# Attention, gated layers and an expert layer on one core: other PSUM banks for the weight fold, two engines to empty the products with v, longer runs in the first loads, and a new plan

## The chip, the cores and the metric

The kernel runs on one core of a Trainium2 chip. The metric is the device time of one execution in microseconds (us). The kernel before was timed three times, and one more execution was profiled.

## What is computed

The reference has three parts, one behind the other.

```python
# attention, batch 4, 12 heads, 448 rows, 64 columns
scores = cap * tanh(scale * q @ k.T / cap)
x = softmax(scores) @ v                 # 1792 x 768 after the heads are put together
# dense part
h = (x @ w1) * (x @ w2) @ w3            # 768 -> 1024 -> 1024
x = h @ w_out                           # 1024 -> 768
# experts: one of 8 for each row, chosen by x @ w_gate + bias[modality]
out = gate * (max(x @ w1[e], 0) @ w2[e])
```

The weights of the dense part come in 64-bit floats and are narrowed on the chip by four integer steps on VectorE.

## The kernel before, in words

There are two stages.

**The planned stage** holds attention and the preparation of the dense weights. Attention works on 24 pairs of heads. For a pair, `load_k`, `load_q` and `load_v` (lines 432 to 447) fetch the rows; k and q go through SyncE's queue (the first q through ScalarE's), v through GpSimd's. In `load_k` and `load_q` the innermost run is one row of 64 floats, 256 bytes. `tr_k` and `tr_q` transpose on TensorE into a PSUM bank of the tag `tr`, which has two banks; `k_out` and `q_out` copy from there. `score` (line 481) writes two banks of the tag `sc`, which has two buffers of two banks; ScalarE applies tanh out of PSUM and then exp. `pv` (line 500) accumulates products with v in the one buffer `pv` of two banks: its two banks hold two halves of the keys, and their sum is the result. `pv_copy` (line 545) copies the first bank to SBUF on ScalarE, and behind it `pv_out` (line 549) adds the second bank on VectorE; `pair_store` writes it to DRAM. `psum` (line 520) adds the exponentials on VectorE and `sum_mm` adds over partitions on TensorE into an `sc` buffer, which `sum_out` copies.

The dense weights: w_out arrives in 8 pieces, is narrowed (`abs1`, `narrow1`), split in a high and a low part (`cast1`, and `sub1` on GpSimd, line 329), and each piece is transposed (`tr_wo`, copied by `wo_copy`) for a product with w_gate (`wo_gate`, read by `wo_split`, line 594), all through `tr` banks. w3 arrives in 16 pieces, is narrowed (`abs_w3`, `conv_w3`) and transposed (`tr_w3`). `fold` (line 635) multiplies w3 with w_out so that the dense part's last two products become one: 16 pieces of two halves, 12 matmuls each. Both halves of a piece share one `sc` buffer, and `fold_out` (line 652) takes each from there to SBUF on VectorE. Some pieces of w1 and w2 are narrowed and stored in this stage too. 30 transposes of the identity (lines 748 to 751) fill TensorE's first microseconds; they hold one `tr` bank until the last of them.

The order of the instructions on each engine is made when the program is built, by the class `Schedule` (line 20), a list scheduler. Each task has an engine or a choice of engines, a cost in ns, a key (its due time, in quarters of a pair), tasks it depends on, and buffers it takes and gives back in rotation; a load has a time on the DMA queue (`dma`). Of the ready tasks the one that can start first is taken, and among equals the one with the smaller key. A TensorE task of the same kind as the one before (64x64 tiles, or full array) has its key lowered by 2.5 (line 85). These costs and keys only make the order; on the chip each engine follows its own order and waits for its true inputs and buffers. GpSimd's order holds the subtractions of line 329 and the issues of `load_v`.

**The second stage** (from line 964 on) is written out by hand: `phase_x12` multiplies x with w1 and w2, both parts of x (high, index 0, and low, index 1) with the high and low parts of the weights, for six slices of the contraction in turn: high by high, low by high, high by low (lines 1000 to 1002). `phase_x2` and the experts (`stage1`, `stage2`) follow. The split of the first x into high and low parts (lines 933 and 935) lies at the end of the planned stage.

Of the kernel before, what the change touches and what calls it, by code (L numbers as in the profile page):

```python
# [8 lines left out]
F32 = mybir.dt.float32  # L9
# [10 lines left out]
class Schedule:  # L20
# [34 lines left out]
    def run(self):  # L55
# [8 lines left out]
        while ready:  # L64
            best = None
            for i in ready:
# [54 lines left out]
def attention_moe_moe_kernel(  # L121
# [292 lines left out]

    raw_qkv = {}

# [15 lines left out]
    def load_k(p):  # L432
        k2 = at2.tile([P, NC, 2, D], F32, name="k2", tag="k2")
        q2 = at2.tile([CP, NC, 2, D], F32, name="q2", tag="q2")
        raw_qkv[p] = (k2, q2)
        for g in range(2):
            nc.sync.dma_start(k2[rows_of(g), 0:NC - g], keys(heads(k, p), g).rearrange("h p c d -> p c h d"))

    def load_q(p):
        eng = nc.sync if p else nc.scalar  # L440
        eng.dma_start(raw_qkv[p][1], heads(q, p).rearrange("h (p c) d -> p c h d", c=NC))

# [102 lines left out]
    def pv_copy(p):  # L545
        pvs[p] = at1.tile([P, S], F32, name="pvs", tag="pvs", bufs=2)
        nc.scalar.copy(pvs[p], pvb[p][:, 0, :S])

    def pv_out(p):
        nc.vector.tensor_tensor(out=pvs[p], in0=pvb[p][:, 1, :S], in1=pvs[p], op=ALU.add)  # L550

    def pair_store(p):
        b, hp = divmod(p, H // 2)
        nc.sync.dma_start(xb[b][P * hp:P * hp + P, :], pvs[p])

# [224 lines left out]
    for c in range(NW):  # L780
        u = c // 2
        key = (4.0 * c + 3) if c < 8 else (10 + 10.0 * c)
        raw, y, un = ("wraw", c), ("y", c), ("unit", u)
# [8 lines left out]
        if c < 8:  # L792
# [3 lines left out]
            for j in range(2):  # L796
                x = add("PE", 320, kg, do(tr_wo, c, j), [cn3[-1], *gate[-1:], *cps[-1:]], take=[tt[j], *([] if j else [("th", "o", c)])], use=[tt[j], y, ("th", "o", c)])
                cps.append(add({'ACT': (500, -300), 'DVE': (560, 0)}, 0, kg, lambda eng, c=c, j=j: wo_copy(c, j, eng), [x], use=[tt[j], ("th", "o", c)]))
            gate.append(add("PE", 1500, kg, do(wo_gate, c), [*cps, wg_in], take=[tp], use=[tp, ("th", "o", c)]))
# [21 lines left out]
    for p in range(NP + 1):  # L821
# [17 lines left out]
        if p:  # L839

            for c in range(3):
                vl[p - 1, c] = add("PE", 770, 4 * p + c + 2.4, do(pv, p - 1, c), [ex[c], joint, vl.get((p - 1, c - 1))],
                                   use=[pk, ("th", p - 1, c), ("v", p - 1)], mode="tiles")
# [51 lines left out]
    for n, (f, g) in enumerate(SWEEP):  # L895
        key = 5.4 * (n + 2) + 3
        raw, r_, h_, w_ = ("w3raw", n), ("w3r", n), ("tr", "w", n), ("w3t", n)
        t = add("SP", 630, key - 3, do(load_w3, n), take=[raw], use=[raw], dma=1456)
        t = add({'ACT': (660, -300), 'DVE': (610, 0)}, 0, key, lambda eng, n=n: abs_w3(n, eng), [t], take=[r_], use=[raw, r_])
# [3 lines left out]
        t = add("PE", 440, key, do(tr_w3, n), [t], take=[h_], use=[r_, h_])  # L903
        t = add({'DVE': (598, 0), 'ACT': (480, 600)}, 0, key - 4, lambda eng, n=n: w3_h(n, eng), [t], take=[w_], use=[h_, w_])
        wl_[n] = t = add("DVE", 600, key - 4, do(w3_l, n), [t], use=[h_, w_])
        lp = add("SP", 630 if g else 0, key - 3, do(part, n), [fs[n - KF]] if g else [], take=[("wst", n)], use=[("wst", n)],
                 lag=0, dma=1092 if g else None)
        for half in range(2):
            fo = ("sc", "f", n)
            late = vl[NP - 2, 2] if n == FN - 1 else None  # L910
            prev = add("PE", 2130, FK(n, half), do(fold, n, half), [t, units[2 * g], units[2 * g + 1], *augs[4 * g:4 * g + 4], prev, late],
                       take=[] if half else [fo], use=[fo, w_, ("unit", 2 * g), ("unit", 2 * g + 1)])
            fe[n, half] = add("DVE", 560, 0, do(fold_out, n, half), [prev, lp], use=[fo, ("wst", n)])
# [74 lines left out]
    def phase_x12(half, bs, hooks):  # L988
        gt = gp.tile([P, 2, KF, HALF], F32R, name="gT", tag="gT")
        units = {}  # L990
        for i, (u, j) in enumerate(ORDER[half]):
# [357 lines left out]
```

## Time and profile before

| quantity | us |
|---|---|
| three timed runs | 958.78, 961.33, 965.59 |
| median | 961.33 |
| the profiled execution | 963.59 |
| its span in the profile | 961.7 |

The profiled execution's own time is 963.59 us. The span runs from its first to its last instruction; 1.9 us lie around it. The profile names engines PE (TensorE's matmuls), PEld (its weight loads), DVE (VectorE), ACT (ScalarE), POOL (GpSimd) and SP (SyncE). Matmuls are pipelined: a row's duration is the way of one matmul through the array, and the next one starts before it ends, so that PE looks busy where matmuls start at half the possible rate. What the engine really does is read from the distance of starts.

### The profile page before, as it was taken

How to read it: one execution, taken by the hardware profiler on the slowest of the kernel's cores; microseconds unless marked ns; L12 is line 12 of the kernel's file. 1: busy time of each engine (PE TensorE's matmuls, PEld its weight loads, DVE VectorE, ACT ScalarE, POOL GpSimd, SP SyncE). 2: the span in 40 equal slices, each digit the busy share in tenths (PEclk: the TensorE clock that was granted, in tenths of full speed). 3: DMA queues.
4: the chain of work that ended last, by engine and by line, in shares of the span. 5: the costliest groups of instructions: out<-in, count | busy, mean ns of one | idle time of the engine just before them, and what ended most of it. 6: DMA issues, size and time to landing. Idle time of an engine off the chain costs nothing. (4 is left out here: it accounts for less than half of the span.)

```text
span 961.7 us, 13900 instructions
## 1 busy us (share of the span) xinstructions
PE 924.1 (96%) x5618; PEld 763.5 (79%) x5618; DVE 469.1 (49%) x671; ACT 374.9 (39%) x447; POOL 241.0 (25%) x211
## 2 busy tenths in 40 slices
PE   8999989999999999999999999999999999999994
PEld 5456555655655799999999999999899899889894
DVE  4999986786675478721006422100653523423410
ACT  4897766776775333231222211211422312322400
POOL 3434211151110112123542441200604212302011
PEclk9899999999999999999999999999999999999998
DMA  9767785477544565626622341310671591782401
GB/s 225 206 167 219 203 243 141 129 217 179 156 140 121 146 193 164 186 79 215 171 93 96 78 120 34 115 50 33 166 178 43 184 172 33 199 148 52 160 20 44
DMA packets 126088, 132.73 MB, mean 138 GB/s; under 512 B 60926, under 2 KB 107416, under 8 KB 126021
## 3 DMA queue, kind: packets, MB, share of 16 engines
q1 hardware_dynamic: 112644, 114.35, 42.3%
q0 software_dynamic: 12464, 17.22, 7.9%
q8 instruction: 46, 0.75, 0.3%
q10 hardware_dynamic: 912, 0.23, 0.1%
q14 instruction: 22, 0.17, 0.1%
HBM read 102.13 MB, written 30.19 MB: 138 GB/s over the span
## 5 line engine op out<-in xcount | busy, mean ns | idle before, releaser
L1001 PE MATMUL acc<-xT,wh 128*128 128x448 f32 x384 | 141.4, 368 | 0.7 <-DVE xT L935 0.7
L1000 PE MATMUL acc<-xT,wh 128*128 128x448 f32 x384 | 140.4, 366 | 1.5 <-ACT xT L933 1.5
L1002 PE MATMUL acc<-xT,wl 128*128 128x448 f32 x384 | 140.4, 366 | 0.0
L329 DVE TENSOR_TENSOR wl<-raw,wh 128x1536 fp32r<-128x1536 f32 (+1 forms) x42 | 73.6, 1759 | 116.8 <-ACT wh L252 116.8
L252 ACT CAST wh<-raw 128x1536 fp32r<-128x1536 f32 (+1 forms) x48 | 70.3, 1479 | 105.4 <-DMA raw<-in_moe_w_dram 78.5
L487 PE MATMUL sc<-QT,KT 64*64 64x448 f32 x672 | 92.9, 561 | 7.9 <-ACT smt L252 4.2
L507 PE MATMUL pv<-th,vt 64*64 64x448 f32 x672 | 89.2, 551 | 0.0
L498 ACT ACTIVATE th<-th,capb 128x448 f32<-128x448 f32 (+1 forms) x96 | 89.0, 956 | 0.6
L1214 PE MATMUL acc<-wh,hT 128*124 128x384 f32 x256 | 87.8, 343 | 1.1 <-DVE y L1222 0.7
L447 POOL DMA_DIRECT2D vt<-in_v_dram x96 | 50.9, 545 | 146.3 <-PE pv L507 144.9
L1216 PE MATMUL acc<-wh,hT 128*124 128x384 f32 x256 | 86.5, 338 | 0.7 <-DVE hT L1185 0.7
L1215 PE MATMUL acc<-wl,hT 128*124 128x384 f32 x256 | 86.3, 337 | 0.5 <-DVE wl L329 0.5
L1010 POOL TENSOR_TENSOR gT<-a,gT 128x896 fp32r<-128x896 f32 x16 | 43.8, 2740 | 144.2 <-DVE gT L1009 138.7
L1000 PEld LDWEIGHTS acc<-xT,wh 128*128 128x128 f32 x384 | 72.5, 189 | 8.2 <-ACT xT L933 2.3
L1001 PEld LDWEIGHTS acc<-xT,wh 128*128 128x128 f32 x384 | 72.6, 189 | 7.0 <-DVE xT L935 1.2
L492 ACT ACTIVATE th<-sc,icap 128x896 f32<-128x896 f32 x72 | 71.2, 1010 | 16.2 <-PE sc L487 15.6
L1002 PEld LDWEIGHTS acc<-xT,wl 128*128 128x128 f32 x384 | 72.6, 189 | 5.3
L1032 PE MATMUL acc<-wh,gT 128*128 128x388 f32 x224 | 76.4, 341 | 0.0
L1033 PE MATMUL acc<-wl,gT 128*128 128x388 f32 x224 | 76.0, 339 | 0.0
L1034 PE MATMUL acc<-wh,gT 128*128 128x388 f32 x224 | 75.9, 339 | 0.0
L1180 PE MATMUL acc<-xsT,wh 128*128 128x496 f32 x192 | 74.9, 390 | 0.0
L1182 PE MATMUL acc<-xsT,wl 128*128 128x496 f32 x192 | 74.5, 388 | 0.0
(163 smaller groups left out, 1630.1 us busy)
## 6 DMA issues: line engine op xcount, KB each, us to landing
raw<-in_moe_w_dram SPq DMA_DIRECT2D x48, 768.0 KB
w3raw<-in_moe_w_dram SPq DMA_DIRECT2D x16, 512.0 KB
raw<-w_scr SPq DMA_DIRECT2D x8, 776.0 KB
raw<-in_moe_w_out_dram SPq DMA_DIRECT2D x8, 768.0 KB
w_scr<-y SPq DMA_DIRECT2D x16, 384.0 KB
raw<-w_scr SPq DMA_DIRECT2D x8, 768.0 KB
x_scr<-pvs SPq DMA_DIRECT2D x24, 224.0 KB
xraw<-x_scr SPq DMA_DIRECT2D x4, 1344.0 KB
```

The source lines that it names most:

```text
L487: mm(sc[rows_of(side(p, j, g)), g, :S], lhsT=KT[p][rows_of(j), o:o + D], rhs=QT[p][rows_of(j), :], start=True, stop=True)
L498: nc.scalar.activation(tht[p, c], tht[p, c], ACTF.Exp, scale=capb)
L507: mm(pvb[p][rows_of(j), r, :S], lhsT=vt[p][rows_of(r), NC * g + c, :], rhs=tht[p, c][rows_of(r), g, :] if c < NB else tht[p, c][rows_of(r) ...
L1000: mm(acc[:, ft, :S], lhsT=wh[:, o:o + P], rhs=x[:, 0, d, :], start=(d == 0), stop=False)
L1001: mm(acc[:, ft, :S], lhsT=wh[:, o:o + P], rhs=x[:, 1, d, :], start=False, stop=False)
L1002: mm(acc[:, ft, :S], lhsT=wl[:, o:o + P], rhs=x[:, 0, d, :], start=False, stop=(d == KD - 1))
L1032: mm(acc[:, hf, :HA], lhsT=gt[:, 0, f, ts], rhs=wh[:, o:o + HA], start=(f == 0), stop=False)
L1033: mm(acc[:, hf, :HA], lhsT=gt[:, 0, f, ts], rhs=wl[:, o:o + HA], start=False, stop=False)
L1034: mm(acc[:, hf, :HA], lhsT=gt[:, 1, f, ts], rhs=wh[:, o:o + HA], start=False, stop=(f == KF - 1))
L1214: mm(acc[:TP, hf, :HT], lhsT=ht[:, 0, f, cs], rhs=wh[:, o:o + HT], start=(f == 0), stop=False)
L1215: mm(acc[:TP, hf, :HT], lhsT=ht[:, 0, f, cs], rhs=wl[:, o:o + HT], start=False, stop=False)
L1216: mm(acc[:TP, hf, :HT], lhsT=ht[:, 1, f, cs], rhs=wh[:, o:o + HT], start=False, stop=(f == KF - 1))
```

## The change

The fold takes one `tr` bank for each half in place of an `sc` buffer for both. `pvs` has two halves: ScalarE copies one bank of `pv`, the new `pv_copy1` copies the other on VectorE, and `pv_out` adds the two in SBUF on GpSimd. For the first two pairs k and q are loaded head by head with four rows in a run (1024 bytes; 768 for the shorter part of k) into tiles of the tag `th`, and `order_k` (two copies on VectorE) and `order_q` (one on ScalarE) bring them into the old order. In `phase_x12` the products with the low part of x come after the others of a slice of columns. Keys, costs and dependences of the plan change.

```diff
                 if pick[2] == "PE" and self.tasks[i][9] == mode:
-                    key -= 2.5
+                    key -= 1.7
...
+        if p < NF:
+            runs[p] = [at1.tile([P, 2, NC, D], F32, name="run", tag="th", bufs=7) for _ in range(2)]
         for g in range(2):
-            nc.sync.dma_start(k2[rows_of(g), 0:NC - g], keys(heads(k, p), g).rearrange("h p c d -> p c h d"))
+            n, src = NC - g, keys(heads(k, p), g)
+            if p < NF:
+                nc.sync.dma_start(runs[p][0][rows_of(g), :, 0:n], src.rearrange("h p c d -> p h c d"))
+            else:
+                nc.sync.dma_start(k2[rows_of(g), 0:n], src.rearrange("h p c d -> p c h d"))
...
+    def order_k(p):
+        for g in range(2):
+            n = NC - g
+            nc.vector.tensor_copy(raw_qkv[p][0][rows_of(g), 0:n], runs[p][0][rows_of(g), :, 0:n].rearrange("p h c d -> p c h d"))
+
+    def order_q(p):
+        nc.scalar.copy(raw_qkv[p][1], runs[p][1][0:CP].rearrange("p h c d -> p c h d"))
...
     def pv_copy(p):
-        pvs[p] = at1.tile([P, S], F32, name="pvs", tag="pvs", bufs=2)
-        nc.scalar.copy(pvs[p], pvb[p][:, 0, :S])
+        pvs[p] = at1.tile([P, 2, S], F32, name="pvs", tag="pvs", bufs=2)
+        nc.scalar.copy(pvs[p][:, 0, :], pvb[p][:, 0, :S])
+
+    def pv_copy1(p):
+        nc.vector.tensor_copy(pvs[p][:, 1, :], pvb[p][:, 1, :S])
 
     def pv_out(p):
-        nc.vector.tensor_tensor(out=pvs[p], in0=pvb[p][:, 1, :S], in1=pvs[p], op=ALU.add)
+        nc.gpsimd.tensor_tensor(out=pvs[p][:, 0, :], in0=pvs[p][:, 0, :], in1=pvs[p][:, 1, :], op=ALU.add)
...
-        if half == 0:
-            both = psa.tile([P, 2, 512], F32, name="sc", tag="sc", bufs=2)
-            fos[n, 0], fos[n, 1] = both[:, 0, :], both[:, 1, :]
-        fo = fos[n, half]
+        fo = fos[n, half] = bank("tr", 2)
...
-        key = (4.0 * c + 3) if c < 8 else (10 + 10.0 * c)
+        key = (6.0 * c + 3) if c < 8 else (10 + 10.0 * c)
...
-                cps.append(add({'ACT': (500, -300), 'DVE': (560, 0)}, ... do wo_copy
+                cps.append(add({'ACT': (500, 600), 'DVE': (560, 0)}, ... do wo_copy
...
-            lk = add("SP", 1260, k0, do(load_k, p), take=[raw], use=[raw], dma=640)
-            lq = add("SP" if p else "ACT", 630, k0 + 0.1, do(load_q, p), [(lk, 0)] if p else [], use=[raw], dma=640)
-            lv = add("POOL", 2800, k0 + 4.0, do(load_v, p), [(lk, 0)], take=[vk], use=[vk], dma=640)
-            t = add("PE", 380, 4 * p - 5.2, do(tr_k, p), [lk], take=[hk], use=[hk, raw])
+            lk = add("SP", 1260, k0, do(load_k, p), ..., dma=700 if first else 2300)
+            lq = add("SP" if p else "ACT", 630, k0 + 0.1, do(load_q, p), ..., dma=700 if first else 2300)
+            if first:
+                lk = add("DVE", 1050, kk, do(order_k, p), [lk], use=[raw, rk])
+                lq = add("ACT", 620, kk, do(order_q, p), [lq], use=[raw, rq])
+            t = add("PE", 380, 4 * p - 4.2, do(tr_k, p), [lk], take=[hk], use=[hk, raw])
...
+            lv = add("POOL", 2500, k0 + 4.0, do(load_v, p), [lk], take=[vk], use=[vk], dma=900)
...
-                vl[p - 1, c] = add("PE", 770, 4 * p + c + 2.4, do(pv, p - 1, c), ...
+                vl[p - 1, c] = add("PE", 770, 4 * p + c + 0.8, do(pv, p - 1, c), ...
...
-            po[p - 1] = add("DVE", 620, 4 * p - 2, do(pv_out, p - 1), [t], use=[pk, ("pvs", p - 1)])
+            t1 = add("DVE", 620, 4 * p - 2, do(pv_copy1, p - 1), [(t, -500)], use=[pk, ("pvs", p - 1)])
+            po[p - 1] = add("POOL", 1200, 4 * p - 2, do(pv_out, p - 1), [t, t1], use=[("pvs", p - 1)])
...
-        key = 5.4 * (n + 2) + 3
+        key = 4.6 * (n + 2) + 3
...
-        t = add({'ACT': (660, -300), 'DVE': (610, 0)}, 0, key, ... abs_w3
+        t = add({'ACT': (660, 0), 'DVE': (610, 0)}, 0, key, ... abs_w3
...
-            fo = ("sc", "f", n)
+            fo = ("tr", "f", n, half)
...
-                    for d in range(KD):
-                        o = d * 256 + ft * P
-                        mm(acc[:, ft, :S], lhsT=wh[:, o:o + P], rhs=x[:, 0, d, :], start=(d == 0), stop=False)
-                        mm(acc[:, ft, :S], lhsT=wh[:, o:o + P], rhs=x[:, 1, d, :], start=False, stop=False)
-                        mm(acc[:, ft, :S], lhsT=wl[:, o:o + P], rhs=x[:, 0, d, :], start=False, stop=(d == KD - 1))
+                    for part in range(2):
+                        for d in range(KD):
+                            o = d * 256 + ft * P
+                            mm(acc[:, ft, :S], lhsT=wh[:, o:o + P], rhs=x[:, part, d, :], start=(d == part == 0), stop=(part == 1 and d == KD - 1))
+                            if part == 0:
+                                mm(acc[:, ft, :S], lhsT=wl[:, o:o + P], rhs=x[:, 0, d, :], start=False, stop=False)
```

## Rows read from the trace of the kernel before

**Rows 1.** Busy time of each engine in stretches, with instruction counts, granted clock, DMA.

```profile
core 0: us, PE busy (x) PEld busy (x) DVE busy (x) ACT busy (x) POOL busy (x), PEclk, DMA share, GB/s
...
20.00:40.00 20.00, 18.77 (x158) 8.72 (x155) 18.64 (x27) 18.25 (x26) 7.70 (x10) 0.91 0.78 216
40.00:60.00 20.00, 19.30 (x165) 9.74 (x169) 19.73 (x30) 18.55 (x27) 7.21 (x7) 0.91 0.67 180
60.00:140.00 80.00, 76.13 (x610) 48.98 (x606) 72.24 (x116) 57.87 (x80) 24.70 (x30) 1.00 0.78 211
140.00:160.00 20.00, 16.86 (x137) 9.96 (x130) 15.13 (x24) 13.71 (x19) 2.80 (x6) 0.91 0.47 147
160.00:300.00 140.00, 134.45 (x1110) 80.61 (x1110) 97.06 (x150) 101.57 (x130) 31.33 (x58) 1.00 0.61 170
...
315.20:320.00 4.80, 4.13 (x11) 3.46 (x12) 3.08 (x3) 1.63 (x2) 0.00 (x0) 0.64 0.83 260
320.00:949.50 629.50, 626.20 (x3258) 584.90 (x3257) 228.62 (x299) 148.04 (x149) 158.93 (x83) 1.00 0.43 118
```

**Rows 2.** Timeline of PE, 238.5 to 255: start, us, form, count.

```profile
238.91 0.98 PE L487 MATMUL sc<-QT,KT 64*64 64x448 f32 x8 [0.53 <-DVE wst L655]
...
245.09 0.60 PE L474 MATMUL tr<-ident,q 112*128 112x112 f32 x4
245.46 0.42 PE L648 MATMUL sc<-wh,w3h 128*128 128x388 f32 x1
...
249.87 0.98 PE L534 MATMUL sc<-sums,sel 64*64 64x448 f32 x8
```

**Rows 3.** Waits of PE, 14 to 317: who, for whom, us in total, times, longest.

```profile
PE sc L487 <- ACT smt L252: 4.2, 3, 3.1
PE tr L619 <- DVE wl L598: 1.9, 2, 1.3
PE acc L1000 <- ACT xT L933: 1.5, 1, 1.5
PE sc L487 <- ACT th L495: 1.4, 2, 0.7
PE sc L648 <- DVE wst L657: 1.4, 2, 1.0
PE sc L487 <- DVE wst L655: 1.3, 3, 0.6
...
PE acc L1001 <- DVE xT L935: 0.7, 1, 0.7
```

**Rows 4.** Timeline of ACT and of PE, 140.5 to 145.

```profile
141.93 0.89 ACT L224 ACTIVATE y<-raw 128x768 f32<-128x768 f32 x1 [3.61 <-DMA raw<-in_moe_w_dram]
...
144.59 0.59 PE L487 MATMUL sc<-QT,KT 64*64 64x448 f32 x2 [3.15 <-ACT smt L252]
```

**Rows 5.** Timeline of PE, 7 to 14.

```profile
7.24 1.17 PE L460 MATMUL tr<-ident,k 128*128 128x128 f32 x4 [2.46 <-DMA k<-in_k_dram]
8.34 3.67 PE L750 MATMUL tr<-ident 128*128 128x128 f32 x16
11.81 0.95 PE L474 MATMUL tr<-ident,q 112*128 112x112 f32 x4
```

**Rows 6.** Groups of VectorE's instructions in the planned stage, by shape.

```profile
L550 DVE TENSOR_TENSOR pvs<-pv,pvs 128x448 f32<-128x448 f32 x24 | 14.8, 615 | 5.5 <-ACT pvs L547 4.3 <-DMA w3raw<-in_moe_w_dram 1.0
...
L254 DVE COPY KT<-tr 128x448 f32<-128x448 f32 x16 | 9.9, 618 | 2.8 <-PE tr L460 1.8 <-PE sc L487 0.9
```

**Rows 7.** Timeline of GpSimd and of VectorE, 33.3 to 37.

```profile
33.95 1.97 POOL L329 TENSOR_TENSOR wl<-y,wh 128x768 fp32r<-128x768 f32 x1 [6.20 <-ACT wh L252]
...
34.16 2.24 DVE L527 TENSOR_TENSOR sums<-sums,th 128x448 f32<-128x448 f32 x1
```

**Rows 8.** Durations of single lines, ns min/median/max, first and last start in us.

```profile
L527 DVE TENSOR_TENSOR sums<-sums,th x24: 608/617/2242, 24.4 to 310.5; 128x448 f32<-128x448 f32 x24
...
L329 POOL TENSOR_TENSOR wl<-y,wh x14: 1811/1920/2656, 23.7 to 212.1; 128x768 fp32r<-128x768 f32 x14
```

More of the change, by code (lines that the diff above doesn't have):

```diff
@@ L413, in attention_moe_moe_kernel @@
     nc.gpsimd.memset(sel, 1.0)
-    raw_qkv = {}
+    raw_qkv, runs = {}, {}
+    NF = 2
     def rows_of(r):
@@ L435, in load_k @@
         raw_qkv[p] = (k2, q2)
+        if p < NF:
+            runs[p] = [at1.tile([P, 2, NC, D], F32, name="run", tag="th", bufs=7) for _ in range(2)]
         for g in range(2):
-            nc.sync.dma_start(k2[rows_of(g), 0:NC - g], keys(heads(k, p), g).rearrange("h p c d -> p c h d"))
-    def load_q(p):
-        eng = nc.sync if p else nc.scalar
-        eng.dma_start(raw_qkv[p][1], heads(q, p).rearrange("h (p c) d -> p c h d", c=NC))
+            n, src = NC - g, keys(heads(k, p), g)
[3 more added lines that the diff above has]
+                nc.sync.dma_start(k2[rows_of(g), 0:n], src.rearrange("h p c d -> p c h d"))
+    def load_q(p):
+        src = heads(q, p)
+        if p < NF:
+            eng = nc.sync if p else nc.scalar
+            eng.dma_start(runs[p][1][0:CP], src.rearrange("h (p c) d -> p h c d", c=NC))
+        else:
+            nc.sync.dma_start(raw_qkv[p][1], src.rearrange("h (p c) d -> p c h d", c=NC))
+    def order_k(p):
[4 more added lines that the diff above has]
+        nc.scalar.copy(raw_qkv[p][1], runs[p][1][0:CP].rearrange("p h c d -> p c h d"))
     def load_v(p):
@@ L797, in attention_moe_moe_kernel @@
                 x = add("PE", 320, kg, do(tr_wo, c, j), [cn3[-1], *gate[-1:], *cps[-1:]], take=[tt[j], *([] if j else [("th", "o", c)])], use=[tt[j], y, ("th", "o", c)])
-                cps.append(add({'ACT': (500, -300), 'DVE': (560, 0)}, 0, kg, lambda eng, c=c, j=j: wo_copy(c, j, eng), [x], use=[tt[j], ("th", "o", c)]))
+                cps.append(add({'ACT': (500, 600), 'DVE': (560, 0)}, 0, kg, lambda eng, c=c, j=j: wo_copy(c, j, eng), [x], use=[tt[j], ("th", "o", c)]))
             gate.append(add("PE", 1500, kg, do(wo_gate, c), [*cps, wg_in], take=[tp], use=[tp, ("th", "o", c)]))
@@ L828, in attention_moe_moe_kernel @@
             k0, kk = 4 * p - 7, 4 * p - 4.0
-            lk = add("SP", 1260, k0, do(load_k, p), take=[raw], use=[raw], dma=640)
-            lq = add("SP" if p else "ACT", 630, k0 + 0.1, do(load_q, p), [(lk, 0)] if p else [], use=[raw], dma=640)
-            lv = add("POOL", 2800, k0 + 4.0, do(load_v, p), [(lk, 0)], take=[vk], use=[vk], dma=640)
-            t = add("PE", 380, 4 * p - 5.2, do(tr_k, p), [lk], take=[hk], use=[hk, raw])
+            first = p < NF
+            rk, rq = [("th", "run", p, i) for i in range(2)] if first else [None] * 2
+            lk = add("SP", 1260, k0, do(load_k, p), take=[raw, rk, rq] if first else [raw], use=[raw, rk] if first else [raw], dma=700 if first else 2300)
+            lq = add("SP" if p else "ACT", 630, k0 + 0.1, do(load_q, p), [(lk, 0)] if p else [], use=[raw, rq] if first else [raw], dma=700 if first else 2300)
+            if first:
+                lk = add("DVE", 1050, kk, do(order_k, p), [lk], use=[raw, rk])
+                lq = add("ACT", 620, kk, do(order_q, p), [lq], use=[raw, rq])
+            t = add("PE", 380, 4 * p - 4.2, do(tr_k, p), [lk], take=[hk], use=[hk, raw])
             kl = add({'DVE': (620, 0), 'ACT': (530, 300)}, 0, kk, lambda eng, p=p: k_out(p, eng), [t], take=[kt], use=[hk, kt])
             t = add("PE", 380, 4 * p - 5.2, do(tr_q, p), [lq], take=[hq], use=[hq, raw])
+            lv = add("POOL", 2500, k0 + 4.0, do(load_v, p), [lk], take=[vk], use=[vk], dma=900)
             last_at2.append(t)
@@ L841, in attention_moe_moe_kernel @@
             for c in range(3):
-                vl[p - 1, c] = add("PE", 770, 4 * p + c + 2.4, do(pv, p - 1, c), [ex[c], joint, vl.get((p - 1, c - 1))],
+                vl[p - 1, c] = add("PE", 770, 4 * p + c + 0.8, do(pv, p - 1, c), [ex[c], joint, vl.get((p - 1, c - 1))],
                                    use=[pk, ("th", p - 1, c), ("v", p - 1)], mode="tiles")
@@ L895, in attention_moe_moe_kernel @@
     for n, (f, g) in enumerate(SWEEP):
-        key = 5.4 * (n + 2) + 3
+        key = 4.6 * (n + 2) + 3
         raw, r_, h_, w_ = ("w3raw", n), ("w3r", n), ("tr", "w", n), ("w3t", n)
         t = add("SP", 630, key - 3, do(load_w3, n), take=[raw], use=[raw], dma=1456)
-        t = add({'ACT': (660, -300), 'DVE': (610, 0)}, 0, key, lambda eng, n=n: abs_w3(n, eng), [t], take=[r_], use=[raw, r_])
+        t = add({'ACT': (660, 0), 'DVE': (610, 0)}, 0, key, lambda eng, n=n: abs_w3(n, eng), [t], take=[r_], use=[raw, r_])
         t = add({'DVE': (500, 0)}, 0, key, lambda eng, n=n: conv_w3(n, 0, eng), [t], use=[raw, r_])
@@ L902, in attention_moe_moe_kernel @@
             t = add("DVE", (0, 425, 690, 910)[i], key, do(conv_w3, n, i), [t], use=[raw, r_])
-        t = add("PE", 440, key, do(tr_w3, n), [t], take=[h_], use=[r_, h_])
-        t = add({'DVE': (598, 0), 'ACT': (480, 600)}, 0, key - 4, lambda eng, n=n: w3_h(n, eng), [t], take=[w_], use=[h_, w_])
+        t = add("PE", 440, key, do(tr_w3, n), [t], take=[h_, w_], use=[r_, h_, w_])
+        t = add({'DVE': (598, 0), 'ACT': (480, 600)}, 0, key - 4, lambda eng, n=n: w3_h(n, eng), [t], use=[h_, w_])
         wl_[n] = t = add("DVE", 600, key - 4, do(w3_l, n), [t], use=[h_, w_])
@@ L908, in attention_moe_moe_kernel @@
         for half in range(2):
-            fo = ("sc", "f", n)
+            fo = ("tr", "f", n, half)
             late = vl[NP - 2, 2] if n == FN - 1 else None
             prev = add("PE", 2130, FK(n, half), do(fold, n, half), [t, units[2 * g], units[2 * g + 1], *augs[4 * g:4 * g + 4], prev, late],
-                       take=[] if half else [fo], use=[fo, w_, ("unit", 2 * g), ("unit", 2 * g + 1)])
+                       take=[fo], use=[fo, w_, ("unit", 2 * g), ("unit", 2 * g + 1)])
             fe[n, half] = add("DVE", 560, 0, do(fold_out, n, half), [prev, lp], use=[fo, ("wst", n)])
```

2 lines of the change are left out of this document (1 added, 1 removed).

## The prediction

> **What bounds the kernel now.** The first view to read is the busy time in stretches. In the second stage TensorE has work in 626.2 of 629.5 us at a granted clock of 1.00 [rows 1]: nothing that the change touches there takes a matmul away, so the second stage stays as long as it is. The planned stage ends at 315.2 us, and all that can be won lies in it. There the busy column deceives. The timeline shows it: from 238.91 to 245.09 TensorE starts 64 tile matmuls, and from 245.46 to 249.87 the 24 matmuls of a fold piece [rows 2], though single rows there show 0.3 to 1 us. So a dense tile matmul costs 6.18 / 64 = 0.097 us and a fold matmul 4.41 / 24 = 0.184 us. The stage has 1536 tile matmuls (24 pairs by 28 + 28 + 8), 384 of the fold (16 by 24) and 400 small ones (transposes and products with w_gate). By the dense rate that is 1536 x 0.0966 = 148.3, 384 x 0.184 = 70.6, and for the small ones 400 x 0.12 = 48, an estimate, since four transposes of q take 0.37 [rows 2] and those of k reach further. Together 267 us. The first transposes of q start at 11.81 [rows 5]; from there to 315.2 are 303 us. About 36 us of the stage are therefore lost on TensorE, and this is the pot.
>
> Two views say where they go. First the clock: in 20:40, 40:60 and 140:160 it was granted at 0.91 [rows 1], each time a part of the stretch at the lower of the two levels, 1.2 GHz; that is (1 - 0.91) x 20 = 1.8 us of work each, 5.4 together. Before the one at 140:160 TensorE had stood for 3.15 us [rows 4]. Second the list of waits: scores waiting for a free `sc` buffer, behind `sum_out` 4.2, behind tanh 1.4, behind `fold_out` 1.3, and folds waiting for one 1.4, sum 8.3; transposes waiting for a `tr` bank 1.9; and the stage's end, 1.5 and 0.7 [rows 3]. What is left of the pot, some 18 us, is spread over many short gaps, mostly where the engine changes between tiles and the full array. VectorE is the second limit early on: 18.64 and 19.73 of 20 us in two stretches and 72.24 of 80 in the next, but 97.06 of 140 after 160 [rows 1].
>
> **The change part by part**, against the profiled execution's own 963.59 us.
>
> *Fold in the transposes' banks.* No instruction is added. A score no longer waits for a fold to leave its buffer, nor a fold for a score. Of the 8.3 us, 3.15 fell in one place: ScalarE stood 3.61 us for a load of raw weights, in front of the copy that frees the buffer [rows 4]. The plan had that load earlier than it came, and loads of k and q were charged with 640 there; the change charges 2300, so that instructions that need a load come later in the order. I take all of the 8.3 as gone: -8.3. At the ends: nothing, if other waits take their place, and -8.3. What is late next is the `tr` bank: each half holds one for 12 x 0.184 = 2.2 us, and for `fold_out` behind it, some 0.54 us (an estimate, 388 of the 448 columns of a 0.618 us copy, rows 6). A transpose that comes straight behind two halves waits for that. Before, waits for a `tr` bank were 1.9 [rows 3]; I take them as growing by 1.5. At the ends: 0, where tiles follow each fold as in rows 2, and 16 pieces by 0.9 (the copy and two signals, an estimate) = +14.4.
>
> *Two engines empty the products with v.* VectorE's `pv_out` was 0.615 us; a copy of the same size out of PSUM is 0.618 [rows 6]: no change in VectorE's sum. The `pv` buffer comes free some 0.6 us sooner, but no wait of TensorE on it is in the list, so 0. The add goes to GpSimd. The trace has no such add on it; the nearest row is the subtraction of 768 columns, 1.811 to 2.656 us, median 1.920 [rows 8], so 448 columns are 1.06 to 1.55 us and by the median 1.12 (estimates). The add waits for both copies; behind it on GpSimd stand loads of v and subtractions. Loads of v have three buffers ahead, and that cover hides the add; without it each pair would be later by up to 1.55. What it does to VectorE is the dearer question. When GpSimd's subtraction ran from 33.95 to 35.92, an addition on VectorE of usually 0.617 us took 2.24 and ended half a microsecond behind it [rows 7, 8]. So the added 24 x 1.12 = 27 us of GpSimd can cost VectorE between nothing and 27 us, as much as the 14 x 1.92 = 27 us of subtractions could before. Those show up on TensorE, at worst, as the 1.9 us behind `wo_split` [rows 3]; I take a like price, rounded down since most of the 24 adds fall after 140 us where VectorE has air: +1.5. At the ends: 0 and +27; of the upper end most would fall into the 43 us that VectorE has left of 160:300 [rows 1], and the part that wouldn't is the third rival's price.
>
> The Trainium skill, GPSIMD Engine Reference, section 1 (Specifications), says that GpSimd shares its SBUF interfaces with VectorE, and that those VectorE instructions collide that have two SBUF inputs or run in a two-port mode. The trace agrees for the addition, which has two SBUF inputs [rows 7]. By that rule taken alone every one of the 24 adds would strike an instruction of the saturated VectorE; this is the third rival below.
>
> *First loads in long runs.* The first k was waited for 2.46 us; then 16 transposes of the identity, 3.47 us to the next start, stood between the transposes of k and those of q [rows 5]. Long runs bring k and q earlier, but two copies on VectorE and one on ScalarE now lie between. The copies are new, 512 and 384 floats a lane for k and 512 for q; the nearest row is 0.618 for 448 [rows 6], so about 0.71 + 0.53 = 1.24 for k and 0.7 for q (estimates), for two pairs, on engines that have little to do then: that idle time hides the second pair's, and without it they cost 1.24. The first q can't be transposed before the identity's bank is free, and more of those 16 now run ahead of k. I take -1.5. At the ends: +1.2, when k lands no earlier and is then copied, and -2.5, the whole wait.
>
> *Order in the first product of the second stage.* The low part of x is needed six slices later: the wait of 0.7 for it [rows 3] goes, -0.7. Its ends: 0 and -0.7. Elsewhere in the second stage the same matmuls run in another order: 0.
>
> *The clock.* With the long stand at 141 gone and the early stage smoother I take two of the three low stretches as gone: -3.6. At the ends 0 and -5.4; the low stretch at the start of the second stage (0.64 in 4.8 us, 1.7 us) stays, since the stand of 1.5 in front of it stays.
>
> *Keys of the plan.* The pieces of w_out come later (6 in place of 4 quarters apart) and those of w3 earlier, which takes load off VectorE in 20:60. Their effect is in the terms above; alone 0, ends -5 (a part of the 18 us of short gaps) and +5, if the lower bonus for staying in one mode adds changes of mode.
>
> Sum: -8.3 + 1.5 + 1.5 - 1.5 - 0.7 - 3.6 = -11.1, so 952.5 for an execution such as the profiled one. That one lay 2.3 above the median of the runs (961.33); a median is therefore expected at 950.2.
>
> **The rivals.**
> - *The waits only change their name.* TensorE is almost dense from 160 to 300, and short gaps at mode changes are the larger part of the pot; a new order keeps them. Then only start and end gain: 961.33 - 1.5 - 0.7 = 959.1. For it speaks that the 18 us are in no list of waits; against it that 8.3 plus 5.4 are, and that the changed buffers are just those.
> - *The `tr` banks become the bound.* With every piece of the fold followed by a transpose: +14.4 in place of +1.5, so 950.2 + 12.9 = 963.1. Against it: in rows 2 tiles follow the fold.
> - *GpSimd holds VectorE.* Of the 24 adds some 10 fall in 20:140 (120 of 290 us), where VectorE is busy over 90% [rows 1]. Each of these lands on an instruction of VectorE, at the long end of the price, 10 x 1.55 = 15.5 on the path, with no gain in the waits or the clock (the copies that free `sc` and `tr` come later) and only the start's and the end's 2.2: 961.33 + 15.5 - 2.2 = 974.6. It decides against the change from 11.1 + 1.5 = 12.6 us of holds on the path if the other gains stay, or from 2.2 if they don't. The hold of 1.6 us in rows 7 speaks for it, the low load of VectorE after 160 against it. The rule named above is this mechanism.
> - *The long runs bring nothing*: 951.7, inside the forecast's own range.
>
> **How the numbers follow.** The forecast has 0.54, the unchanged waits 0.23, the `tr` banks 0.08, the holds 0.15. What a measurement of this kernel can tell from no change is about 1%, 9.6 us, that is 951.7 and 970.9. The forecast's own range is 940 to 957: 0.45 of its 0.54 lies below 951.7, 0.09 above. With 0.01 of the second case, faster is 0.46. Same: 0.09 + 0.22 + 0.06 + 0.02 = 0.39; slower: 0.13 + 0.02 = 0.15. Below, the range reaches to 940: all ends taken together would be -8.3 - 2.5 - 0.7 - 5.4 - 5 = -21.9, which is 939.4. Above it reaches to 966, over the second and third cases; most of the holds' case and a few hundredths below are left out.
>
> **What would show it.** Right: the second stage's start moves from 315.2 to about 304, at an unchanged length behind; scores waiting on `fold_out`, and folds on `sc`, are gone from the list; no stretch at 140:160 below 1.00; first q transposes before 10.5; GpSimd's adds of 1.1 to 1.3 us. Wrong: transposes waiting for `fold_out` by more than 4 us in total; additions of line 527 whose median leaves 0.617 us, or instructions of VectorE stretched as in rows 7 in every pair; a stage end later than 312. A second stage of another length than 634 would refute the premise.

## The result, and the profile after

| | kernel before | changed kernel |
|---|---|---|
| runs | 19 | 19 |
| median, us | 965.08 | 957.58 |
| lowest to highest, us | 958.78 to 971.64 | 950.01 to 962.54 |
| profiled execution, us | 963.59 | 950.01 |
| its span, us | 961.7 | 948.2 |

The ratio is 0.9913, with a 95% interval of 0.9889 to 0.9937: 0.9% faster. A second measurement of the same kernel, in the last group of experiments, gave 0.9934 (0.9908 to 0.9961). The forecast was 950.2 from 961.33, a ratio of 0.988: sign and size are near. In us, 957.58 lies just above the forecast's own range of 940 to 957, since the kernel before was slower here too (965.08 for 961.33); 0.9913 of 961.33 would be 953.0. The profiled execution of the changed kernel is the fastest of its 19 runs, so its trace shows what happens, and the ratios say how much.

The planned stage ends 8.6 us sooner in this execution, at 306.61 instead of 315.21. The timeline of PE in the changed kernel (start, us, form, count, idle before), first the start and then the seam of the stages:

```profile
7.22 0.75 PE L479 MATMUL tr<-ident,k 128*128 128x128 f32 x4 [1.51 <-DVE k L457]
7.90 1.20 PE L769 MATMUL tr<-ident 128*128 128x128 f32 x9
8.94 0.55 PE L493 MATMUL tr<-ident,q 112*128 112x112 f32 x4
...
10.87 2.69 PE L506 MATMUL sc<-QT,KT 64*64 64x448 f32 x20
...
306.61 0.47 PE L1027 MATMUL acc<-xT,wh 128*128 128x448 f32 x1 [1.86 <-ACT xT L958]
```

The first q are transposed at 8.94 instead of 11.81 [rows 5], since fewer transposes of the identity stand between k and q (9 for 16) and each takes less time in this execution: from 7.90 to 8.94 are 1.04 us for the 9, where the 16 took 3.47. k itself comes to TensorE no sooner: 7.22 after 7.24.

PE's waits of the changed kernel from 12 to 307 (who, for whom, us in total, times, longest):

```profile
PE tr L641 <- DVE wst L676: 3.4, 2, 1.8
PE tr L614 <- DVE woT L254: 2.9, 3, 1.1
PE acc L1027 <- ACT xT L958: 1.9, 1, 1.9
PE sc L506 <- ACT th L511: 1.4, 2, 0.8
PE tr L606 <- DVE w3l L649: 1.0, 1, 1.0
...
PE tr L493 <- DVE woT L254: 0.9, 2, 0.5
PE tr L493 <- DVE wst L674: 0.8, 1, 0.8
PE tr L606 <- DVE y L244: 0.6, 1, 0.6
```

Against [rows 3]: of the 8.3 us for the scores' buffers 1.4 are left, behind tanh alone. In their place stand waits that all end with VectorE, each in front of an instruction that writes a transposes' bank: 3.4 + 2.9 + 1.0 + 0.9 + 0.8 + 0.6 = 9.6. Of these 6.1 wait for the bank to be emptied (4.2 for `fold_out`, lines 674 and 676), and 3.5 for an input that VectorE hadn't made yet (woT, 2.9, and y, 0.6). The same sum before was 4.3 and not only the 1.9 of [rows 3]; the list there goes on, beside one more of 0.3, with

```profile
PE tr L592 <- DVE KT L254: 1.2, 1, 1.2
...
PE tr L460 <- DVE wl L598: 0.9, 1, 0.9
```

The wait of 0.7 for the low part of x is gone.

Stretches of the changed kernel (columns as in [rows 1]):

```profile
20.00:40.00 20.00, 19.16 (x179) 9.98 (x182) 19.36 (x28) 18.75 (x26) 9.91 (x12) 1.00 0.74 211
40.00:60.00 20.00, 17.80 (x159) 8.73 (x151) 19.35 (x26) 18.26 (x26) 9.38 (x12) 1.00 0.60 183
60.00:140.00 80.00, 76.41 (x601) 47.40 (x601) 76.40 (x111) 60.81 (x79) 31.84 (x36) 0.98 0.64 187
140.00:160.00 20.00, 17.41 (x137) 10.87 (x135) 17.89 (x26) 10.70 (x15) 5.21 (x7) 1.00 0.64 188
160.00:300.00 140.00, 137.53 (x1139) 83.34 (x1142) 113.04 (x158) 107.91 (x140) 44.24 (x67) 1.00 0.63 179
```

The clock holds at 1.00 in three stretches where it was 0.91 [rows 1], in this execution, and is 0.98 in 60:140, where it was 1.00. But VectorE is busier everywhere after 60 us, 76.40 for 72.24 and 113.04 for 97.06, though it has hardly more to do. Its instructions are stretched. The durations of the first addition of a pair's exponentials (L542), of VectorE's new copy out of PSUM (L569) and of GpSimd's addition (L572), ns min/median/max:

```profile
L542 DVE TENSOR_TENSOR sums<-th x24: 1075/1750/3979, 16.9 to 297.8; 128x896 f32<-128x896 f32 x24
...
L569 DVE COPY pvs<-pv x24: 607/624/626, 23.5 to 302.2; 128x448 f32<-128x448 f32 x24
...
L572 POOL TENSOR_TENSOR pvs<-pvs x24: 1143/1176/1913, 24.1 to 302.9; 128x448 f32<-128x448 f32 x24
```

An addition that takes 1.08 us has a median of 1.75. One place shows why; the timelines of VectorE and of GpSimd in the changed kernel, 68 to 73.5:

```profile
69.38 3.47 DVE L542 TENSOR_TENSOR sums<-th 128x896 f32<-128x896 f32 x1
...
68.97 1.15 POOL L572 TENSOR_TENSOR pvs<-pvs 128x448 f32<-128x448 f32 x1
70.06 1.83 POOL L329 TENSOR_TENSOR wl<-y,wh 128x768 fp32r<-128x768 f32 x1
```

GpSimd's two instructions last from 68.97 to 71.89, and VectorE's addition ends at 72.85, 0.96 us behind them, a little less than its own 1.08: it hadn't been slowed, it had been kept waiting for both. The two timelines over the whole stage say the same. 16 of the 24 first additions are stretched, and each of the 16 ends 0.95 to 0.97 us behind the last instruction of GpSimd that it met; 14 had met one of the new additions, two only a subtraction. Once it is the other way round: GpSimd's longest addition, 1.913 us, lies beside a first addition of VectorE that runs from 297.85 to 298.93 unstretched, and ends 0.99 us behind it.

The copy out of PSUM never exceeds 0.626. The Trainium skill, GPSIMD Engine Reference, section 1 (Specifications), names VectorE instructions with two SBUF inputs or in a two-port mode as those in contention with GpSimd. The rows of L542, with two SBUF inputs, and of L569, with none, agree.

The two banks aren't emptied at once either. The groups of VectorE in the planned stage (count, busy us, mean ns, idle before), the first line from the kernel before (L523 is the first addition there) and the others from the changed kernel; then the timelines of ScalarE and VectorE, 166 to 172, in the changed kernel:

```profile
L523 DVE TENSOR_TENSOR sums<-th 128x896 f32<-128x896 f32 x24 | 26.7, 1114 | 4.2 <-ACT th L498 4.2
...
L542 DVE TENSOR_TENSOR sums<-th 128x896 f32<-128x896 f32 x24 | 47.2, 1965 | 1.3 <-ACT th L517 1.2
...
L569 DVE COPY pvs<-pv 128x448 f32<-128x448 f32 x24 | 14.9, 620 | 15.3 <-ACT pvs L566 15.3
```

```profile
168.65 0.52 ACT L566 COPY pvs<-pv 128x448 f32<-128x448 f32 x1
...
169.26 0.62 DVE L569 COPY pvs<-pv 128x448 f32<-128x448 f32 x1 [0.63 <-ACT pvs L566]
```

VectorE stood 15.3 us in all for ScalarE's copy, and in each of the 24 pairs its own began after the other's end, at the least 0.03 us behind. The order counted on 500 ns of overlap. Whether two tiles in place of the two halves of one would let the copies run side by side wasn't tried.

### The profile page after: what moved, and what is told of

Read it like the earlier page. It is cut to its first block, busy times and chain, and to the rows that moved or that the text cites. A ratio compares the mean times of both kernels' runs of the same rounds, so it can differ in the third digit from the quotient of the medians.

```text
span 948.2 us, 13934 instructions
## 1 busy us (share of the span) xinstructions
PE 916.9 (97%) x5618; PEld 758.8 (80%) x5618; DVE 492.0 (52%) x673; ACT 379.6 (40%) x451; POOL 266.1 (28%) x235
## 5 line engine op out<-in xcount | busy, mean ns | idle before, releaser
L1027 PE MATMUL acc<-xT,wh 128*128 128x448 f32 x768 | 218.5, 365 | 2.6 <-ACT xT L958 2.6
L1207 PE MATMUL acc<-xsT,wh 128*128 128x496 f32 x192 | 74.9, 390 | 0.0
L1208 PE MATMUL acc<-xsT,wh 128*128 128x496 f32 x192 | 73.8, 385 | 0.0
L1267 POOL DMA_INDIRECT out_dram<-y,idx x15 | 23.7, 1577 | 137.0 <-DVE y L1263 136.4
```

The costliest lines, as they stand in the source:

```text
L1027: mm(acc[:, ft, :S], lhsT=wh[:, o:o + P], rhs=x[:, part, d, :], start=(d == part == 0), stop=(part == 1 and d == KD - 1))
L1207: mm(acc[:, ft, :T], lhsT=wh[:, o:o + P], rhs=xt[:, 0, d, :], start=(d == 0), stop=False)
```

## The experiments

All ratios are to the kernel before, which ran beside each group on the same chip. An edit is against the changed kernel unless said otherwise.

**GpSimd's addition left out, the order kept.**

```diff
     def pv_out(p):
-        nc.gpsimd.tensor_tensor(out=pvs[p][:, 0, :], in0=pvs[p][:, 0, :], in1=pvs[p][:, 1, :], op=ALU.add)
+        pass
```

> The changed kernel with its plan and order kept, but GpSimd's addition of the two halves of the products with v is not emitted (the attention output is then only half of the keys' sum). If the additions' hold of VectorE costs time (theory: VectorE stretched by some 21 us in 18 of 24 first additions of exponentials, about 10 pairs in the stretch where it is over 90% busy), the planned stage ends 4 to 8 us sooner and the ratio to the kernel before falls from 0.991 to 0.983 to 0.987. If VectorE's spare time hides the hold (rival), the stage's end moves by less than 2 us and the ratio stays at 0.989 to 0.993.

Ratio 0.9744 (0.9694 to 0.9794), median 940.9: a larger gain than even the first theory asked for. The planned stage ends at 295.98, 10.6 us sooner than in the changed kernel's trace (16.7 sooner than in its second trace, shown further down), with the same order on every engine. PE's waits at the transposes' banks, from 12 us on, shrink, in this run, to

```profile
PE tr L606 <- DVE w3l L649: 0.6, 1, 0.6
PE tr L493 <- DVE woT L254: 0.4, 1, 0.4
...
PE tr L641 <- DVE wst L674: 0.2, 1, 0.2
```

and two more of 0.2, one of them behind ScalarE. So most of the 9.6 us weren't the price of putting the fold there; they were VectorE being late. The stretches show it too, the first of the changed kernel and the other two of this run:

```profile
20.00:160.00 140.00, 130.78 (x1069) 76.98 (x1068) 133.00 (x188) 108.52 (x143) 56.34 (x65) 0.99 0.65 190
...
20.00:160.00 140.00, 138.82 (x1164) 82.85 (x1160) 130.05 (x205) 115.35 (x153) 42.77 (x55) 1.00 0.68 199
...
60.00:140.00 80.00, 79.99 (x648) 50.07 (x647) 75.05 (x121) 62.97 (x84) 24.29 (x30) 1.00 0.67 197
```

PE starts 648 matmuls in 60:140 instead of 601, and VectorE finishes 121 instructions in 75.05 us instead of 111 in 76.40. From 20 to 160, where VectorE has 133.00 of 140 us of work in the changed kernel, PE's idle time falls from 9.2 to 1.2 us; from 160 to the stage's end it is 4.3 and 3.3. So the holds cost where VectorE is nearly full, and later its spare time hides most of them.

The stage from 12 us on, in the kernel before and in this run:

```profile
12.00:315.21 303.21, 285.48 (x2318) 167.96 (x2316) 235.37 (x363) 223.99 (x296) 73.73 (x109) 0.98 0.65 180
...
12.00:295.98 283.98, 278.86 (x2309) 164.54 (x2307) 234.90 (x360) 226.59 (x298) 71.81 (x109) 1.00 0.68 192
```

**GpSimd busy as long, but reading nothing.**

```diff
     def pv_out(p):
-        nc.gpsimd.tensor_tensor(out=pvs[p][:, 0, :], in0=pvs[p][:, 0, :], in1=pvs[p][:, 1, :], op=ALU.add)
+        nc.gpsimd.iota(pvs[p][:, 1, :].bitcast(I32), pattern=[[1, S]], base=0, channel_multiplier=1)
+        nc.gpsimd.iota(pvs[p][:, 1, :].bitcast(I32), pattern=[[1, S]], base=0, channel_multiplier=1)
```

> The changed kernel with its plan and order kept; GpSimd's addition is replaced by two number ramps written into the second half of the same tile, about as long together as the 1.18 us addition (the attention output then holds half of the keys' sum). GpSimd still waits for VectorE's copy and is busy, but reads nothing. If the addition costs by holding VectorE, VectorE's first additions go back to about 1.1 to 1.3 us and the ratio to the kernel before falls to 0.972 to 0.980, as without the addition. If it costs by keeping GpSimd's queue (loads of v and subtractions later), the ratio stays at 0.986 to 0.993.

Ratio 0.9759 (0.9720 to 0.9797), as without the addition. The groups of GpSimd in this run (count, busy us, mean ns, idle before):

```profile
L572 POOL IOTA pvs<- 128x448 int32 x24 | 12.9, 537 | 24.1 <-DVE pvs L569 24.0
L573 POOL IOTA pvs<- 128x448 int32 x24 | 12.6, 523 | 1.6
```

and VectorE's first addition, ns min/median/max:

```profile
L542 DVE TENSOR_TENSOR sums<-th x24: 1077/1084/2728, 17.2 to 288.3; 128x896 f32<-128x896 f32 x24
```

GpSimd spends 1.06 us on each pair here, for 1.18 before, and waits for VectorE's copy in the same place; yet VectorE's median is back at 1.084. The cost is the hold, not GpSimd's queue. (The longest, 2.728, is left; the 14 subtractions still run.)

**The old emptying of the products with v.**

```diff
-        pvs[p] = at1.tile([P, 2, S], F32, name="pvs", tag="pvs", bufs=2)
-        nc.scalar.copy(pvs[p][:, 0, :], pvb[p][:, 0, :S])
+        pvs[p] = at1.tile([P, S], F32, name="pvs", tag="pvs", bufs=2)
+        nc.scalar.copy(pvs[p], pvb[p][:, 0, :S])
...
-        nc.gpsimd.tensor_tensor(out=pvs[p][:, 0, :], in0=pvs[p][:, 0, :], in1=pvs[p][:, 1, :], op=ALU.add)
+        nc.vector.tensor_tensor(out=pvs[p], in0=pvb[p][:, 1, :S], in1=pvs[p], op=ALU.add)
```

> The changed kernel with the old emptying of the products with v (a copy on ScalarE, then the addition out of PSUM on VectorE), the plan made anew. If the early release of that buffer is worth something (theory of the change), the ratio to the kernel before rises to 0.995 to 1.000. If it is worth nothing and the hold costs (rival), it falls to 0.983 to 0.989. If both are small, 0.989 to 0.994.

Ratio 0.9742 (0.9700 to 0.9785), median 941.33, lower than the theory of the hold had asked for. This version beats both kernels, by 2.6% and, as 0.9742 to 0.9913, by 1.7%. Its plan is another one, but its ratio is that of the run above, which kept the order; an accident of the order is unlikely. The `pv` buffer isn't freed earlier by the new way, as the copies' timeline shows, and nothing is lost by the old one; VectorE's addition out of PSUM (groups of VectorE in this run) costs

```profile
L569 DVE TENSOR_TENSOR pvs<-pv,pvs 128x448 f32<-128x448 f32 x24 | 14.7, 611 | 1.1 <-ACT pvs L566 0.9
```

0.611 us a pair, what the copy costs that replaced it.

**The fold back in a score buffer.**

```diff
-        fo = fos[n, half] = bank("tr", 2)
+        if half == 0:
+            both = psa.tile([P, 2, 512], F32, name="sc", tag="sc", bufs=2)
+            fos[n, 0], fos[n, 1] = both[:, 0, :], both[:, 1, :]
+        fo = fos[n, half]
...
```

> The changed kernel with the fold back in one buffer of scores for both halves, the plan made anew. If the banks are the gain (my prediction's largest term, 8.3 us), the waits for a score buffer come back and the ratio to the kernel before is 0.998 to 1.003. If the waits only moved from the scores' buffers to the transposes' banks (rival: 8.3 us named there before, 9.8 at the others after), it stays at 0.989 to 0.994.

Ratio 1.0169 (1.0121 to 1.0217): above both expectations, and 25 us above the changed kernel, three times the whole of my term. PE's waits say that not all of it is the buffers' own price:

```profile
PE sc L553 <- DVE sums L546: 10.9, 1, 10.9
PE sc L670 <- DVE wst L679: 3.8, 4, 2.0
PE sc L506 <- DVE smt L254: 2.6, 1, 2.6
```

The waits for score buffers are back (3.8, 2.6, 2.1 and smaller ones). The single wait of 10.9 us has another origin: in VectorE's order the additions of that pair stand behind a product for the second stage's first x, and that one stood 15.46 us for a load (timeline of VectorE in this run):

```profile
297.83 1.09 DVE L913 TENSOR_TENSOR xraw<-xraw,rb 128x896 f32<-128x896 f32 x1 [15.46 <-DMA rb<-rec_scr]
```

A plan made anew brings its own accidents.

**The old keys, costs and dependences** with the new structure, and **the new ones alone** on the kernel before (of the first's edit three lines; the other keys, costs, DMA times and dependences of the diff go back in the same way):

```diff
-                    key -= 1.7
+                    key -= 2.5
...
-        key = (6.0 * c + 3) if c < 8 else (10 + 10.0 * c)
+        key = (4.0 * c + 3) if c < 8 else (10 + 10.0 * c)
...
-        key = 4.6 * (n + 2) + 3
+        key = 5.4 * (n + 2) + 3
```

> The changed kernel with the old keys, costs, DMA times and dependences of the plan, the new buffers, tail, loads and order of products kept. If the new plan is the gain, the ratio to the kernel before is 0.997 to 1.005. If the structure is the gain, it stays below 0.994.

> The kernel before with the new keys, costs, DMA times and dependences of the plan alone: old banks of the fold, old tail, old loads, old order of products. If the plan is worth something by itself, the ratio to the kernel before is 0.985 to 0.995. If the new keys only fit the new banks (theory after the run with the fold in the scores' buffers, 1.017, and the run with the old keys, 1.004), it is 1.00 to 1.02.

The structure without the keys: 1.0038 (1.0006 to 1.0069). GpSimd's addition is part of that structure and stays in this run, so the ratio doesn't price the banks by themselves. The keys without the structure: 0.9975 (0.9953 to 0.9997), between the two expectations. In the first, the sum on TensorE waited 4.3 us for VectorE's last addition, and products with v waited 4.2 for VectorE's copy, the very wait that this copy was to take away:

```profile
PE sc L553 <- DVE sums L546: 4.3, 2, 3.2
PE pv L526 <- DVE pvs L569: 4.2, 2, 3.6
```

In the second, a fold waited 6.5 us for its score buffer:

```profile
PE sc L667 <- DVE wst L674: 6.5, 1, 6.5
```

**The new banks of the fold alone**, on the kernel before:

```diff
-            fo = ("sc", "f", n)
+            fo = ("tr", "f", n, half)
```

(and `fold` takes `bank("tr", 2)` for each half.)

> The kernel before with one part of the change alone: each half of the fold in a bank of the transposes. If the banks are worth something whatever the plan (8.3 us of waits for the scores' buffers), the ratio to the kernel before is 0.985 to 0.993. If they pay only with the new keys, 0.996 to 1.005.

Ratio 0.9986 (0.9952 to 1.0021): nothing that can be told from no change. The waits only change their place; PE's list has, at folds and transposes,

```profile
PE tr L645 <- ACT KT L252: 2.5, 1, 2.5
PE tr L592 <- DVE KT L254: 1.9, 1, 1.9
```

**Short first loads again**, alone and together with the old tail:

```diff
-    NF = 2
+    NF = 0
...
```

(A second line keeps the first q on ScalarE's queue.)

> The changed kernel with the first two pairs of k and q loaded as before, in runs of 256 bytes, without the copies that order them. If the long runs bring the start forward, the first scores begin 2 to 3 us later than the 10.9 us of the changed kernel and the ratio to the kernel before rises to 0.993 to 0.996. If they bring nothing beyond the start (rival), the ratio stays at 0.988 to 0.993 although the first scores are late.

> The changed kernel with both parts undone that cost time when undone alone made it faster: the old emptying of the products with v (0.974) and the short first loads (0.983); new banks of the fold, new keys and new order of products stay. If the two gains add, the ratio to the kernel before is 0.962 to 0.970. If the gain of the short loads was that of a plan in which fewer of GpSimd's additions fell on VectorE's, nothing is left of it: 0.971 to 0.979.

Alone: 0.9831 (0.9797 to 0.9864). Both my expectations were wrong; the changed kernel is slower than this one, and the first scores begin sooner, at 9.31 instead of 10.87:

```profile
6.46 0.72 PE L479 MATMUL tr<-ident,k 128*128 128x128 f32 x4 [0.91 <-DMA k<-in_k_dram]
...
9.31 1.72 PE L506 MATMUL sc<-QT,KT 64*64 64x448 f32 x12 [0.72 <-DVE QT L254]
```

What the long runs do to the start can't be told from this pair of traces. The first scores begin sooner here because the order differs: 12 of them stand in front of the second pair's transposes, where the changed kernel has all 20 behind. With the keys alone they begin at 9.49, and with the long runs and the old keys at 9.60, for 14.01 in the kernel before. k in short runs is at TensorE at 6.46 here, in long runs and then copied at 7.22 in the changed kernel's first trace but at 6.53 in its second; over all traces it is there at 6.46 to 7.24 with short runs and at 6.20 to 7.22 with long ones. A gain or a price of the long runs isn't shown.

With the old tail the short loads gave 0.9819 (0.9774 to 0.9865), above both expectations and no better than the old tail alone (0.9742), so their gain doesn't add. In the traces the planned stage ends at 298.17 there and at 297.08 with the old tail alone, so most of the difference between the two ratios doesn't lie in the part that was changed. What makes the 0.8% between 0.9831 and 0.9913 stays open; the plan is another, and the medians of VectorE's first additions don't settle it (1.518 us there, 1.750 and 1.568 in the two traces of the changed kernel). The run with the old tail and the short loads answers one more question: besides the order of products it is the kernel before with the new banks and the new keys together, at 0.9819, where the banks alone gave 0.9986 and the keys alone 0.9975.

**The changed kernel once more, and with the old order of products** in the second stage:

```diff
-                            mm(acc[:, ft, :S], lhsT=wh[:, o:o + P], rhs=x[:, part, d, :], start=(d == part == 0), stop=(part == 1 and d == KD - 1))
+                        mm(acc[:, ft, :S], lhsT=wh[:, o:o + P], rhs=x[:, 1, d, :], start=False, stop=False)
...
```

> The changed kernel once more, beside the two others on the same chip. If the short loads' 0.983 is a gain over it, it comes out at 0.988 to 0.994, as in the first measurement (0.991); if chips or runs make up the difference, at 0.981 to 0.986.

> The changed kernel with the old order of the products in the second stage. By my prediction the new order is worth 0.7 us at the seam of the stages: ratio to the kernel before 0.001 above that of the changed kernel, and a wait of the first product with the low part for VectorE is back. A rival: the order changes nothing, since ScalarE's split is waited for either way.

0.9934 (0.9908 to 0.9961) and 0.9944 (0.9915 to 0.9972): 0.001 apart, as expected, and far inside the intervals, so the ratios show nothing. The wait is the witness; with the old order PE's list has again

```profile
PE acc L1026 <- DVE xT L960: 0.7, 1, 0.7
```

The second trace of the changed kernel also shows how much one execution can say. Its span is 958.2 at a mean clock of 0.982, for 948.2 at 0.994, and its stage ends at 312.68. Two stretches of it:

```profile
20.00:60.00 40.00, 36.96 (x310) 18.41 (x308) 35.66 (x52) 33.90 (x47) 16.96 (x22) 0.91 0.65 189
60.00:140.00 80.00, 76.94 (x584) 47.75 (x577) 74.51 (x106) 59.32 (x79) 28.43 (x32) 0.94 0.58 169
```

Waits as before, but the granted clock is at the lower level for 0.09 x 40 + 0.06 x 80 = 8.4 us worth of work, where the first trace lost 0.02 x 80 = 1.6.

**The subtractions moved to VectorE too**, on the old tail:

```diff
-        cs = units[u] = add({'POOL': (1764, 0)}, 0, key, sub, [t], use=[y, un])
+        cs = units[u] = add({'DVE': (1100, 0)}, 0, key, sub, [t], use=[y, un])
```

> The changed kernel with the old emptying of the products with v (0.974) and, besides, the 14 subtractions of the planned stage moved from GpSimd to VectorE, the plan made anew. If a GpSimd instruction holds VectorE for about its own length (14 of 1.9 us) and VectorE needs 1.1 us for the same, the stage gets shorter by up to 10 us: ratio 0.963 to 0.972. If VectorE's time is the limit and the holds fell mostly into its idle time, it gets longer: 0.976 to 0.985.

Ratio 0.9804 (0.9770 to 0.9837) beside 0.9742 (0.9700 to 0.9785): not faster. Whether it is slower isn't settled, since the intervals touch and the planned stage ends at 297.25 beside 297.08. The subtractions on VectorE in this run:

```profile
L329 DVE TENSOR_TENSOR wl<-y,wh 128x768 fp32r<-128x768 f32 x14 | 13.4, 954 | 3.2 <-ACT wh L252 3.2
```

Not every hold is worth removing; here VectorE pays 0.95 us for each 1.9 us of GpSimd, and nothing is won.

## Why the prediction was near, by its own steps

The sum of -11.1 us met a measured gain of some 8 us (0.9913 of 965.08), but the additions' price and the other parts' gain were each wrong by more than that, in opposite directions. That the sum came near is luck. The prediction also gave a gain of more than 1% a chance of 0.46 and a change within 1% one of 0.39; 0.9% is the latter.

- **The addition on GpSimd, +1.5.** This is the step that failed most. It costs 0.9913 - 0.9744 = 1.7%, some 16 us, by both runs that keep the order and take the reading away. The price of one addition was right (1.176 us, from an estimate of 1.12) and so was the mechanism, which stood as the third rival with 0.15 and 15.5 us. The wrong step was to take the 14 subtractions' visible cost for 24 more instructions and round it down for the free time of VectorE. The 24 don't fall at random: 14 meet the first addition of a pair's exponentials, which has two SBUF inputs. Those first additions took 26.7 us before, at a mean of 1.114, and 47.2 after, at 1.965. Behind 160 VectorE's free time did hide most of that, as the prediction said; but 8 of the 16 stretched additions lie in 20:160, and most of the cost arose there. The third rival had this, about ten holds and 15.5 us on the path. What was wrong in it is that nothing else would be gained: the holds went beyond the 12.6 us at which they were to decide against the change, and it won all the same. That the copies don't overlap, and VectorE stands for ScalarE besides, I hadn't seen at all; without the addition this wait stayed (15.3 us), so it isn't the 16 us.
- **The fold's banks, -8.3, the clock, -3.6, and the keys, 0.** Without the addition's cost the other parts are worth 2.6% (0.9742), some 25 us, where the prediction had 12.6 for them (11.1 and the 1.5 of the addition). One by one they can't be credited: the banks alone are worth nothing that can be told (0.9986), the keys alone next to nothing (0.9975), both together 0.9819. The gain is in the pair. The prediction had priced the banks by the waits that they remove and the keys at 0; the runs show that a list of waits prices a buffer only for the order in which it was taken. How the gain divides can be read, for one pair of traces, from the two stretches from 12 us on. The stage ends 19.2 us sooner without the addition than in the kernel before. PE's idle time falls by 12.6 us (17.7 to 5.1), where my terms for waits, -8.3, +1.5 and -0.7, make -7.5: the new order also removed waits further down the list. Its busy time falls by 6.6 us: 1.7 is the start (first scores at 12.33 for 14.01), and the granted clock, 1.00 for 0.98, is enough for the rest, so the clock's term was too small as well. The short gaps that I had taken as fixed stayed: from the first q at 10.07 to 295.98 are 285.9 us, still 19 above the 267 of the dense count. The rest of the 25 us isn't in the planned stage of this pair; its second stage was 3.8 us shorter, and that is within what this stage does by itself (below).
- **Waits at the transposes' banks, +1.5.** They came to 9.6 from 4.3 (the 1.9 that I took was one row of the list), but to 1.4 behind VectorE without the addition. The sign was right and the cause wrong: the holds, not the fold. The waits for `fold_out` alone, 4.2 us, passed the 4 that had been named as a sign of being wrong; they were 2.0 in the second trace and 0.2 without the addition.
- **The start, -1.5.** The first scores came 3.1 us sooner (10.87 for 14.01) in the first pair of traces; with the same order they came between 10.87 and 12.33 in five traces, so the term's sign is met but not its cause. k came at about the same time with either kind of runs. What moved the start isn't separated: the new keys alone (9.49) and the long runs under the old keys (9.60) each go with an early one.
- **The seam, -0.7.** Right, by the wait that goes and comes back; the wait of 1.5 beside it grew to 1.9.
- **The second stage unchanged.** No wait in it answers to the change. In the two profiled executions it was shorter by 948.2 - 306.6 to 961.7 - 315.2, 4.9 us, which by the letter is the sign that was to refute the premise. But with one and the same program this stage took 641.6 to 651.0 us in the traces of the experiments, and 645.5 in the changed kernel's second, so this is the execution's and not the change's. A part of it is the low clock at its start (0.64, [rows 1], 1.7 us), which was missing in the first trace of the changed kernel and back in stretch 300:320 of the second, at 0.91.
- **The other signs.** Of those of being right, 140:160 at 1.00 held in the first trace and not in the second (0.91). Of those of being wrong, the stretched instructions came in 16 of 24 pairs, and the stage's end lay behind 312 in the second trace (312.68).

## What to carry to other kernels

Before work is moved to GpSimd to spare VectorE, look at what VectorE does at that moment: if it reads two operands from SBUF and the two meet, what is left of GpSimd's duration is added to VectorE's, not taken from it, and that costs where VectorE is nearly full. A test that costs little is to keep the order and let GpSimd do something as long that reads nothing. And where an order is planned, buffers and due times are one change: try them together and apart before crediting either, and judge by many runs, since a single trace can lie 1% off.

## What the runs showed of the hardware

- The hold is whole: an addition of 1.08 us on VectorE waited through two GpSimd instructions and took 3.47, ending 0.96 us behind the second. All 16 stretched first additions of the changed kernel end 0.95 to 0.97 us behind GpSimd's last. Who waits can't be read from whose row begins first: at 78.25 VectorE's began 0.33 us before GpSimd's and waited.
- Number ramps on GpSimd, which write 448 columns in 0.537 us without reading any, left VectorE's median at 1.084 us.
- The same kernel ran at mean granted clocks from 0.984 to 0.994 over its 19 runs, and the time went with it: 950.01 us at 0.994, 961.01 at 0.984.
